# Expert matmuls on column strips while attention runs: one tile shape fewer on TensorE

## The chip, the cores and the metric

The kernel runs on one core of a Trainium2 chip. The metric is the device time of one execution in microseconds (us); three executions of the kernel before took 396.23, 396.54 and 396.64 us, median 396.54. One further execution was taken by the hardware profiler, and all profile lines below are of that one. The engines are named as in the profile: PE is TensorE's matmul, PEld its weight load, DVE is VectorE, ACT is ScalarE, POOL is GpSimd (here it issues the loads), SP is SyncE (here it issues the stores).

## The reference

Eight batches with twelve heads of 448 tokens and 64 dimensions go through attention; the heads are joined to rows of 768, and a feed-forward layer ("expert") with one hidden layer of 2,048 and a SiLU follows.

```python
scores = (1/sqrt(64)) * q @ k.transpose(0, 1, 3, 2)        # [8, 12, 448, 448]
attn = softmax(scores, axis=-1)
x = (attn @ v).transpose(0, 2, 1, 3).reshape(3584, 768)
h = x @ w_in                                                # w_in [768, 2048]
g = h / (1 + exp(-h))
out = g @ w_out                                             # w_out [2048, 768], float32
```

Inputs come and the output goes in float32; the kernel computes in fp16 with sums in float32.

## The kernel before, in words

**Attention.** A unit is one batch and one group of four heads (`HG`); batch 0 is cut in two pieces by query, so there are 27 units of 224 or 448 queries. Keys stand in four chunks of up to 128 (`NCH`). `scores` (line 339) computes keys x queries: each head has 64 dimensions, taken as two times 32 rows, and the four heads of the group use the four row strips of the array, tiles of 32x128. ScalarE takes the exponential from PSUM to an SBUF tile `E` (`expo`, line 359).

448 keys are three chunks of 128 and a rest of 64. From unit 7 on, units are worked in pairs (two groups of heads), and the two rests share one chunk: one group lies `low`, its last 64 keys in rows 0 to 63 of chunk 3, the other `high`, in rows 64 to 127 (`form`, `X_TOK`, lines 186 to 261; `load_v` and `turn_k` place V and K so). Scores of the shared rest use tiles of 32x64 (`scores_rest`).

`attend` (line 414) forms, on tiles of 128x32 with one head on each column strip, first the sums of the exponentials (`part` 0, for pairs in `attend_sums`, line 398, with VectorE's sums `T` of the chunks) and then the values, in two parts of 32 of the 64 dimensions. A part of a pair runs for each of its two groups three chunks x four heads of 128x32, and after both groups the shared rest as eight matmuls of 64x32, one half of the rows for each group. `inverse` and `norm` (lines 438 and 468) then write normalised values to `xT` on VectorE.

**Expert.** `ffn1` (line 484) is 6 matmuls of 128x128 against 448 columns (224 for batch 0) into a PSUM bank `h`; ScalarE takes a tanh and VectorE the gate, into `G` (or `X`). The second layer, `product` (line 675), works on two output tiles of 128 tokens at a time with seven products instead of eight, each 8 matmuls of 128x128 against 384 columns; combinations are formed on VectorE (`combine_g`, `combine_w`). The first four output pieces (two tiles, two halves each) are computed plainly (`plain`, line 695). The last two batches' first layer is done in seven products too (`pair_product`, line 603), with buffers of V and E reused for the combinations (`old_buffer`, line 555).

**Order.** A planner at the end of the kernel (lines 763 to 1500) simulates the engines with costs: each piece of work is an `Op` with a cost and what it depends on, `Order.on_pe` (line 106) adds `SWITCH` (0.094) where the tile mode differs from the one before, and rings stand for buffers (`m_ring` for four PSUM banks, `e_ring` for E, `v_ring` for V). TensorE takes score bursts at a pace of 2.6 us, attention where its data are there, and expert work in between. Emitters are collected with their planned time and called in that order, so the planner's times set the order of every engine's queue, and nothing else. `busy`, `mode` and the lines `mms * mm(nq)` in `run_av` (line 1360) are such costs. POOL's loads have a fixed order, given at lines 801 to 827.

V is a tile from a rotating pool with two buffers (`load_v`, line 264): the first load into a buffer waits until all reads of the batch two before are over.

Of the kernel before, what the change touches and what calls it, by code (L numbers as in the profile page):

```python
# [25 lines left out]
def mm(n):  # L26
    return n / 2400.0 + 0.0026
# [37 lines left out]
class Op:  # L65


    def __init__(self, eng, busy, emit, deps=(), bias=0.0, tail=HOP, then=None):
        self.eng, self.busy, self.emit = eng, busy, emit
        self.deps, self.bias, self.tail, self.then = list(deps), bias, tail, then  # L70
        self.done = None
        self.half = False

    def ready(self):
        return when(self.deps)
# [2 lines left out]
class Order:  # L78


    def __init__(self, shy):
        self.now, self.shy = 0.0, shy
        self.free = {"PE": 1.0, "ACT": 2.1, "DVE": 1.2, "POOL": 1.2}
        self.wait = {"ACT": [], "DVE": []}
        self.pool = []
        self.dma_free = 0.0
        self.out = []
        self.mode = None
        self.busy = {e: 0.0 for e in self.free}

    def add(self, op):
# [4 lines left out]
        self.out.append((self.now, len(self.out), fn))  # L96

    def start(self, op):
        self.emit(op.emit)
        self.free[op.eng] = self.now + op.busy  # L100
        self.busy[op.eng] += op.busy
        op.done = self.now + op.busy + op.tail
        if op.then:
            op.then(op.done)

    def on_pe(self, op, mode):
        gap = SWITCH if mode != self.mode else 0.0
        self.mode = mode
        op.busy += gap
        self.start(op)  # L110
# [55 lines left out]
def kernel(  # L166
# [69 lines left out]

    rawk, rawq, KT, QT, VT, E, T, acc, rdn_t, xT, g_t, ost_t = ({} for _ in range(12))
    sT_t, inv_t = {}, {}  # L240
    pS_t = {}

# [19 lines left out]


    def load_v(b, hg0, hg1, x):
        if b not in VT:
            VT[b] = sb.tile([128, NH, NCH, D], FP16, name=f"V_{b}", tag="V", bufs=2)
        hs = slice(HG * hg0, HG * hg1)
        first, count = X_TOK[form(b, hg0)][x]
        nc.gpsimd.dma_start(  # L269
            out=VT[b][32 * x : 32 * (x + 1), hs, 0:count, :],  # L270
            in_=v[b, hs].rearrange("h (i g) d -> i h g d", g=TPP)[
                :, :, first : first + count, :
            ],
        )
# [37 lines left out]
    def turn_q(n):  # L312
        t = rawq[n][:].bitcast(FP32).rearrange("p (g i) -> p g i", i=32)
        nc.vector.transpose(out=t, in_=t)  # L314
        QT[n] = rawq[n].rearrange("p (q e) -> p e q", e=2)

    def score_banks(n, w, ys):
        for y in ys:
# [63 lines left out]
    def attend_mm(a, n, part, c, h, k0, k1, e, start, stop):  # L382
        b, hg, g0, g1 = units[n]
        nq = 32 * (g1 - g0)
        at = nq * (c % per_burst(n))
        if part == 0:
            w = ones[k0:k1, :]
        else:
            w = VT[b][k0:k1, HG * hg + h, c, part - 1 :: 2]
        nc.tensor.matmul(  # L390
            out=a[32 * h : 32 * (h + 1), 0:nq],
            lhsT=w,
            rhs=e[k0:k1, h, at : at + nq],
            start=start,
            stop=stop,
        )
# [15 lines left out]
                )  # L412

    def attend(ns, part):
        made = []
        lone = len(ns) == 1
        if part == 0 and not lone:
            attend_sums(ns)
            return
        for n in ns:  # L420
            a = ps.tile([128, 512], FP32, name=f"a_{n}_{part}", tag="m", bufs=4)
            made.append(a)
            acc[(n, part)] = a
            for c in range(NCH if lone else NCH - 1):
                for h in range(HG):
                    attend_mm(
                        a, n, part, c, h, 0, rows_of(n, c), E[(n, c // per_burst(n))],
                        c == 0, lone and c == NCH - 1,
                    )
        if not lone:  # L430
            for h in range(HG):
                for i, n in enumerate(ns):
                    attend_mm(
                        made[i], n, part, 3, h, 64 * i, 64 * (i + 1), E[(ns[0], 3)],
                        False, True,
                    )

    def inverse(ns, step, i=0):
# [45 lines left out]
    def ffn1(b, f, t0, t1):  # L484
        h = ps.tile([128, 512], FP32, name=f"h_{b}_{f}_{t0}", tag="m", bufs=4)
        for cc in range(NDC):
            nc.tensor.matmul(  # L487
                out=h[:, 0 : t1 - t0],
                lhsT=w_in_t[:, cc, 128 * f : 128 * (f + 1)],
                rhs=x3(b, cc)[:, cc % 3, t0:t1],  # L490
                start=(cc == 0),
                stop=(cc == NDC - 1),
            )
        h_t[(b, f, t0)] = h
# [108 lines left out]
    def pair_product(f, m):  # L603
        if m in (1, 5):
            pp_t[(f, PBANK[m])] = ps.tile(
                [128, 512], FP32, name=f"f_{f}_{m}", tag="m", bufs=4
            )[:, 0:S]
        elif m == 6:
            two = ps.tile([128, 2, 512], FP32, name=f"f_{f}_{m}", tag="s", bufs=2)
            pp_t[(f, "B")], pp_t[(f, "D")] = two[:, 0, 0:S], two[:, 1, 0:S]  # L610
        x = {(r, i): x3(PB + r, 3 * i) for r in range(2) for i in range(2)}
        lo, at = f // 4 * 4, slice(128 * (f % 4), 128 * (f % 4 + 1))
        a, w = {
            1: (x[0, 0], w_in_part(0, 0, f, f + 1)),
            2: (x[0, 1], w_in_part(1, 0, f, f + 1)),
            3: (sx_t.get(4), w_in_part(1, 1, f, f + 1)),
        }.get(m, (None, None))
        if a is None:
            i = {4: 4, 5: 1, 6: 2, 7: 3}[m]
            a, w = x[1, 1] if m == 4 else sx_t[i], tw_t[(i, lo)][:, :, at]  # L620
        for c in range(3):
            nc.tensor.matmul(  # L622
                out=pp_t[(f, PBANK[m])],
                lhsT=w[:, c, :],
                rhs=a[:, c, :],
                start=(c == 0 and m in (1, 6, 5)),
                stop=(c == 2),
                skip_group_check=True,
            )
# [45 lines left out]
    def product(qd, m):  # L675
        a, b = 2 * qd, 2 * qd + 1
        if m in (5, 6):
            w = S_t[(qd, m - 4)]
        else:
            t, i = {1: (a, 0), 2: (a, 1), 3: (a, 1), 7: (b, 0), 4: (b, 1)}[m]  # L680
            w = rows(t, i)
        if BANK[m] == m:
            pr_t[(qd, m)] = ps.tile([128, 512], FP32, name=f"p_{qd}_{m}", tag="m", bufs=4)
        for f in range(HF):
            nc.tensor.matmul(  # L685
                out=pr_t[(qd, BANK[m])][:, 0:OH],
                lhsT=w[:, f, :],
                rhs=W_[m][:, f, :],
                start=(f == 0 and BANK[m] == m),
                stop=(f == HF - 1),  # L690
                skip_group_check=True,
            )


    def plain(t, j, f0, f1):
        if f0 == 0:
            pr_t[("o", t, j)] = ps.tile([128, 512], FP32, name=f"o_{t}_{j}", tag="m", bufs=4)
        for f in range(f0, f1):
            nc.tensor.matmul(  # L699
                out=pr_t[("o", t, j)][:, 0:OH],  # L700
                lhsT=rows(t, f // HF)[:, f % HF, :],
                rhs=B_[f // HF, j][:, f % HF, :],
# [624 lines left out]
    def av_at():  # L1327
# [12 lines left out]
        for n in ns:  # L1340
            if len(exp_op.get(n, ())) < 2 * NCH // per_burst(n):
                return None
            first = 0.0 if n == ns[0] else (NCH - 1) * mm(S)
            for i, x in enumerate(exp_op[n]):
                c = i // 2 * per_burst(n)
                if len(ns) == 2 and c == NCH - 1:
                    c = 2 * (NCH - 1) - (n != ns[0]) * (NCH - 1)
# [12 lines left out]
    def run_av():  # L1360
# [30 lines left out]
        if part == 0:  # L1391
            after_sums(ns, op, nq)
        else:
# [137 lines left out]
```

## Time and profile before

| what | value |
|---|---|
| median of three executions | 396.54 us |
| profiled execution | 396.11 us |
| its span, first to last instruction | 394.3 us |
| TensorE busy | 387.6 us (98%), 3,679 matmuls |
| VectorE / ScalarE busy | 272.7 us (69%) / 253.6 us (64%) |
| granted TensorE clock | 1.000 |
| first layer `h`, 448 columns (line 487) | 480 matmuls, 353 ns mean |
| second layer products (line 685) | 728 matmuls, 326 to 327 ns mean |
| values, 128x32 at 448 columns (line 390) | 496 matmuls, 354 ns mean |
| values, rest, 64x32 (line 390) | 160 matmuls, 360 ns mean |

Matmuls are pipelined: the mean of one is longer than the time from its start to the next one's start, and a busy PE need not be at its peak. So the prediction goes by starts. An entry such as `128*32 128x448` names the tile (rows x columns of the array) and the moving operand (partitions x columns).

The order in time, as the timeline shows it: batch 0's attention alone, on small pieces, up to 30 us; then first-layer work and scores mixed; the last plain output matmul starts at 75.5 us; the last score matmul at 294.9, the last attention matmul at 305.1; after that TensorE has only expert work, up to the end.

### The profile page before, as it was taken

The page shows a single profiled execution, that of the slowest core. Times are in us where ns is not written, and L with a number is a line of the kernel's source. Part 1 is how long each engine was busy: PE and PEld are TensorE (multiplying, and loading weights), DVE is VectorE, ACT ScalarE, POOL GpSimd, SP SyncE. Part 2 cuts the span into 40 slices and gives each one's busy share as a digit, 9 for nine tenths or more (in the row PEclk, how much of TensorE's full clock was granted, in tenths as well). Part 3 has the DMA queues.
Part 4 walks back from the last instruction along what each step waited for, and adds up shares of the span by engine and source line. Part 5 has one row for each costly group of instructions (what it writes and reads, how often), then busy time and mean ns, then how long its engine had stood idle before and what let it go on. Part 6 is the DMA issues. An engine that isn't in the chain of part 4 may idle for free.

```text
span 394.3 us, 9242 instructions
## 1 busy us (share of the span) xinstructions
PE 387.6 (98%) x3679; PEld 200.0 (51%) x3679; DVE 272.7 (69%) x570; ACT 253.6 (64%) x404; POOL 83.6 (21%) x153
## 2 busy tenths in 40 slices
PE   8999999999999999999999999999999999999995
PEld 7667764443444444554444444444444555555563
DVE  2466676999967588963698576896879945457332
ACT  4988885696871986753974759867685236763221
POOL 7532547215001532330006131600000000000000
PEclk9999999999999999999999999999999999999999
DMA  7999999919033946292016683711100130001343
GB/s 116 204 210 210 162 179 187 154 35 141 13 65 79 148 56 86 50 193 62 2 23 90 116 162 52 98 24 31 51 2 7 33 99 25 2 1 29 95 110 90
DMA packets 35579, 34.43 MB, mean 87 GB/s; under 512 B 11600, under 2 KB 34000, under 8 KB 35536
## 3 DMA queue, kind: packets, MB, share of 16 engines
q0 software_dynamic: 24784, 22.82, 38.7%
q1 hardware_dynamic: 9984, 10.24, 9.6%
q10 hardware_dynamic: 768, 0.79, 0.8%
q8 instruction: 29, 0.48, 0.5%
q14 instruction: 14, 0.11, 0.1%
HBM read 45.61 MB, written 11.01 MB: 144 GB/s over the span
## 4 chain that ended last, share of the span: by engine, by line
PE 91%; DVE 4%; ACT 1%; DMA 1%; issue 1%; ACTq 0%; POOL 0%; DVEq 0%; POOLq 0%
PE p L685 28%; PE h L487 28%; PE s L327 12%; PE a L390 10%; PE f L622 8%; PE o L699 3%; PE a L406 2%; DMA rq<-in_q_dram 1%; DVE tw L598 1%; ACT E L364 1%; PE z L1438 1%; DVE G L533 1%; ACTq L734 0%; DVE S L671 0%; DVE G L671 0%
## 5 line engine op out<-in xcount | busy, mean ns | idle before, releaser
L364 ACT ACTIVATE E<-s 128x896 f16<-128x896 f32 (+1 forms) x172 | 149.9, 915 | 22.6 <-PE s L327 21.2
L487 PE MATMUL h<-xT,w_in_t 128*128 128x448 f16 (+1 forms) x672 | 118.9, 327 | 0.0
L487 PEld LDWEIGHTS <-w_in_t 128*128 128x128 f16 x672 | 61.1, 98 | 54.4 <-issue 18.8
L498 ACT ACTIVATE th<-h 128x448 f16<-128x448 f32 (+1 forms) x112 | 54.3, 495 | 31.6 <-PE h L487 21.5
L533 DVE SCALAR_TENSOR_TENSOR G<-th,h 128x448 f16<-128x448 f16 (+2 forms) x112 | 55.1, 507 | 16.0 <-ACT th L498 14.0
L685 PE MATMUL p<-w_out_t,G 128*128 128x384 f16 x368 | 65.3, 326 | 0.3 <-DVE xT L473 0.2
L685 PEld LDWEIGHTS <-G 128*128 128x128 f16 x472 | 45.3, 98 | 33.4 <-issue 4.0
L269 POOL DMA_DIRECT2D V<-in_v_dram x88 | 48.6, 570 | 57.1 <-PE a L390 43.6
L327 PE MATMUL s<-rq,KT 32*128 32x448 f16 (+4 forms) x864 | 56.7, 340 | 0.6 <-ACT E L364 0.4
L742 ACT COPY ost<-p 128x384 f32<-128x384 f32 x39 | 18.7, 479 | 48.5 <-PE p L685 33.5
L390 PE MATMUL a<-E,V 128*32 128x448 f16 (+3 forms) x864 | 40.6, 335 | 0.0
L473 DVE SCALAR_TENSOR_TENSOR xT<-a,rdn 128x448 f16<-128x448 f32 (+1 forms) x54 | 28.9, 568 | 12.5 <-PE a L390 11.7
L254 POOL DMA_DIRECT2D rq<-in_q_dram x27 | 15.2, 561 | 105.2 <-PE s L327 85.8
L685 PE MATMUL p<-D,S 128*128 128x384 f16 x208 | 37.4, 327 | 0.0
L327 PEld LDWEIGHTS <-KT 32*128 32x128 f16 (+2 forms) x864 | 17.5, 98 | 28.7 <-issue 25.9
L390 PEld LDWEIGHTS <-V 128*32 128x32 f16 (+2 forms) x864 | 18.2, 95 | 22.6 <-issue 15.3
L375 DVE TENSOR_TENSOR T<-T,E 128x1792 f16<-128x1792 f16 x20 | 21.7, 1086 | 11.4 <-ACT E L364 11.4
L685 PEld LDWEIGHTS <-S 128*128 128x128 f16 x208 | 19.4, 98 | 16.2 <-issue 3.1
L375 DVE TENSOR_TENSOR T<-E,E 128x1792 f16<-128x1792 f16 x20 | 21.7, 1083 | 7.8 <-ACT E L364 7.8
L647 ACT ACTIVATE G<-f 128x448 f16<-128x448 f32 x32 | 16.2, 547 | 8.4 <-PE f L622 8.3
L304 DVE STREAM_TRANSPOSE KT<-rk 128x256 f32<-128x256 f32 (+3 forms) x48 | 16.6, 384 | 5.9 <-DMA rk<-in_k_dram 5.8
L314 DVE STREAM_TRANSPOSE rq<-rq 128x448 f32<-128x448 f32 (+1 forms) x27 | 15.3, 570 | 6.0 <-DMA rq<-in_q_dram 5.9
(124 smaller groups left out, 323.6 us busy)
## 6 DMA issues: line engine op xcount, KB each, us to landing
out_dram<-ost SPq DMA_DIRECT2D x208, 48.0 KB, 1.6
rk<-in_k_dram POOLq DMA_DIRECT2D x24, 224.0 KB, 4.9
rq<-in_q_dram POOLq DMA_DIRECT2D x21, 224.0 KB, 5.2
w_in_t<-in_moe_w_in_dram POOLq DMA_DIRECT2D x6, 512.0 KB, 11.6
w_out_t<-in_moe_w_out_dram POOLq DMA_DIRECT2D x4, 768.0 KB, 12.9
V<-in_v_dram POOLq DMA_DIRECT2D x43, 64.0 KB, 3.8
V<-in_v_dram POOLq DMA_DIRECT2D x40, 48.0 KB, 3.6
out_dram<-ost ACTq DMA_DIRECT2D x16, 48.0 KB, 1.8
```

The costliest lines, as they stand in the source:

```text
L269: nc.gpsimd.dma_start(out=VT[b][32 * x : 32 * (x + 1), hs, 0:count, :], in_=v[b, hs].rearrange("h (i g) d -> i h g d", g=TPP)[:, :, first ...
L327: nc.tensor.matmul(out=pS[p0 : p0 + 32 * (x1 - x0), h % 2, at : at + nq], lhsT=KT[(b, hg)][32 * h : 32 * (h + 1), c, x0:x1, :, e], rhs=QT[ ...
L364: nc.scalar.activation(out=E[(n, w)][0:kr, 2 * y : 2 * y + 2, 0:nk], in_=pS_t[(n, w, y)][0:kr, :, 0:nk], func=AF.Exp, scale=attn_scale,)
L375: nc.vector.tensor_tensor(out=T[n], in0=T[n] if step else E[(n, 0)], in1=E[(n, step + 1)], op=ALU.add,)
L390: nc.tensor.matmul(out=a[32 * h : 32 * (h + 1), 0:nq], lhsT=w, rhs=e[k0:k1, h, at : at + nq], start=start, stop=stop,)
L473: nc.vector.scalar_tensor_tensor(out=x3(b, cc)[:, cc % 3, 32 * g0 : 32 * g1], in0=acc[(n, part)][:, 0:nq], scalar=0.5, in1=rdn_t[n].rearra ...
L487: nc.tensor.matmul(out=h[:, 0 : t1 - t0], lhsT=w_in_t[:, cc, 128 * f : 128 * (f + 1)], rhs=x3(b, cc)[:, cc % 3, t0:t1], start=(cc == 0), s ...
L498: nc.scalar.activation(out=th, in_=h_t[(b, f, t0)][:, 0 : t1 - t0], func=AF.Tanh)
L533: nc.vector.scalar_tensor_tensor(out=dst[:, f, at + lo : at + hi], in0=th_t[(b, f, t0)][:, lo - t0 : hi - t0], scalar=1.0, in1=h_t[(b, f, ...
L622: nc.tensor.matmul(out=pp_t[(f, PBANK[m])], lhsT=w[:, c, :], rhs=a[:, c, :], start=(c == 0 and m in (1, 6, 5)), stop=(c == 2), skip_group_ ...
L685: nc.tensor.matmul(out=pr_t[(qd, BANK[m])][:, 0:OH], lhsT=w[:, f, :], rhs=W_[m][:, f, :], start=(f == 0 and BANK[m] == m), stop=(f == HF - 1),
L742: nc.scalar.copy(out=ost(qd, i, j), in_=bank(qd, m))
```

## The change

Three things belong together.

1. While attention lasts and the four plain pieces are done (`od.attention`), `on_pe` gives every operation of mode `full` the mode `cols` and marks it `strips`. The new `wide` then issues each of its 128x128 matmuls as four of 128x32, one on each column strip, with the same moving rows. Before and after that, full matmuls stay.
2. The values of a pair no longer take the rest on 64x32 tiles. Chunk 3 is run as any other, 128 rows deep, for both groups, against the shared `E`; the rows that belong to the other group meet zeros in V. A part of a pair has 32 matmuls as before, but eight steps of four where there were six of four and one of eight.
3. V lies in two fixed buffers. `clear_v` puts the zeros in once, by memsets on VectorE: two at the start, three behind batch 0's values and one behind the first pair's. The loads never write these places again, since a head group of a buffer keeps its form from batch to batch.

The planner's costs follow: 8 instead of 7 matmul times for a part of a pair, no mode `rest cols`, other due times for the exponentials of the rest.

```diff
     def start(self, op):
-        self.emit(op.emit)
+        self.emit(lambda: self.run(op))
...
+    def run(self, op):
+        self.strips = op.strips
+        op.emit()
+
     def on_pe(self, op, mode):
+        if mode == "full" and self.attention:
+            mode, op.strips = "cols", True
         gap = SWITCH if mode != self.mode else 0.0
...
+    VT = [const.tile([128, NH, NCH, D], FP16, name=f"V{i}") for i in range(2)]
+
+    def clear_v(i, hg, low):
+        rows = slice(64, 128) if low else slice(0, 64)
+        nc.vector.memset(VT[i][rows, HG * hg : HG * (hg + 1), NCH - 1], 0.0)
+
+    for hg in (1, 2):
+        clear_v(1, hg, hg == 1)
...
     def load_v(b, hg0, hg1, x):
-        if b not in VT:
-            VT[b] = sb.tile([128, NH, NCH, D], FP16, name=f"V_{b}", tag="V", bufs=2)
...
+    def wide(out, lhsT, rhs, **flags):
+        n = 4 if od.strips else 1
+        for j in range(n):
+            at = slice(128 // n * j, 128 // n * (j + 1))
+            nc.tensor.matmul(out=out[at], lhsT=lhsT[:, at], rhs=rhs, **flags)
...
         for n in ns:
             a = ps.tile([128, 512], FP32, name=f"a_{n}_{part}", tag="m", bufs=4)
-            made.append(a)
             acc[(n, part)] = a
-            for c in range(NCH if lone else NCH - 1):
+            for c in range(NCH):
+                e = E[(ns[0] if c == NCH - 1 else n, c // per_burst(n))]
                 for h in range(HG):
                     attend_mm(
-                        a, n, part, c, h, 0, rows_of(n, c), E[(n, c // per_burst(n))],
-                        c == 0, lone and c == NCH - 1,
-                    )
-        if not lone:
-            for h in range(HG):
-                for i, n in enumerate(ns):
-                    attend_mm(
-                        made[i], n, part, 3, h, 64 * i, 64 * (i + 1), E[(ns[0], 3)],
-                        False, True,
+                        a, n, part, c, h, 0, rows_of(n, c), e, c == 0, c == NCH - 1
                     )
...
     def ffn1(b, f, t0, t1):
...
-            nc.tensor.matmul(
+            wide(
...
-            t = sb.tile([128, NH, NCH, D], FP16, name=name, tag="V", bufs=2)
-            t = t.rearrange("p h c d -> p (h c d)")
+            t = VT[name[:2] == "sx"].rearrange("p h c d -> p (h c d)")
...
-            mms = 7 if two else 4
+            mms = 8 if two else 4
...
-            mms * mm(nq) + 0.013 + (0.03 + SWITCH if two and part else 0.0),
+            mms * mm(nq) + 0.013,
...
                     v_ring.give(at)
+                    i = units[ns[-1]][0]
+                    for hg in range(NG if i == 0 else 1 if i == 1 else 0):
+                        low = i == 0 and hg != 1
+                        od.add(
+                            Op("DVE", 0.2, lambda hg=hg, low=low: clear_v(i, hg, low), [op], 5)
+                        )
...
         od.on_pe(op, "cols")
-        if two and part:
-            od.mode = "rest cols"
...
+        od.attention = bool(qk_seq or av_seq) and len(plain_op) == 4
         soon = od.step()
```

The matmul calls in `pair_product`, `product` and `plain` become `wide` as that in `ffn1` does.

More of the change, by code (lines that the diff above doesn't have):

```diff
@@ L72, in __init__ @@
         self.half = False
+        self.strips = False
     def ready(self):
@@ L88, in __init__ @@
         self.mode = None
+        self.strips = False
+        self.attention = True
         self.busy = {e: 0.0 for e in self.free}
@@ L233 @@
     w_out_t = const.tile([128, NFF, DM], FP16, name="w_out_t")
-    rawk, rawq, KT, QT, VT, E, T, acc, rdn_t, xT, g_t, ost_t = ({} for _ in range(12))
+    VT = [const.tile([128, NH, NCH, D], FP16, name=f"V{i}") for i in range(2)]
[4 more added lines that the diff above has]
+        clear_v(1, hg, hg == 1)
+    rawk, rawq, KT, QT, E, T, acc, rdn_t, xT, g_t, ost_t = ({} for _ in range(11))
     sT_t, inv_t = {}, {}
@@ L269, in load_v @@
         nc.gpsimd.dma_start(
-            out=VT[b][32 * x : 32 * (x + 1), hs, 0:count, :],
+            out=VT[b % 2][32 * x : 32 * (x + 1), hs, 0:count, :],
             in_=v[b, hs].rearrange("h (i g) d -> i h g d", g=TPP)[
@@ L388, in attend_mm @@
         else:
-            w = VT[b][k0:k1, HG * hg + h, c, part - 1 :: 2]
+            w = VT[b % 2][k0:k1, HG * hg + h, c, part - 1 :: 2]
         nc.tensor.matmul(
@@ L414, in attend @@
     def attend(ns, part):
-        made = []
         lone = len(ns) == 1
@@ L621, in pair_product @@
         for c in range(3):
-            nc.tensor.matmul(
+            wide(
                 out=pp_t[(f, PBANK[m])],
@@ L684, in product @@
         for f in range(HF):
-            nc.tensor.matmul(
+            wide(
                 out=pr_t[(qd, BANK[m])][:, 0:OH],
@@ L698, in plain @@
         for f in range(f0, f1):
-            nc.tensor.matmul(
+            wide(
                 out=pr_t[("o", t, j)][:, 0:OH],
@@ L1342, in av_at @@
                 return None
-            first = 0.0 if n == ns[0] else (NCH - 1) * mm(S)
+            first = 0.0 if n == ns[0] else NCH * mm(S)
             for i, x in enumerate(exp_op[n]):
                 c = i // 2 * per_burst(n)
-                if len(ns) == 2 and c == NCH - 1:
-                    c = 2 * (NCH - 1) - (n != ns[0]) * (NCH - 1)
                 deps.append((x, first + c * mm(32 * (units[n][3] - units[n][2]))))
```

## The prediction

> **What bounds the kernel now.** I read the page's first part and its chain first, then TensorE's timeline, then the chain of single stretches.
>
> ```profile
> PE 387.6 (98%) x3679; PEld 200.0 (51%) x3679; DVE 272.7 (69%) x570; ACT 253.6 (64%) x404; POOL 83.6 (21%) x153
> ...
> PE 91%; DVE 4%; ACT 1%; DMA 1%; issue 1%; ACTq 0%; POOL 0%; DVEq 0%; POOLq 0%
> ```
>
> TensorE is on the chain for 91% of the span: whatever shortens its own queue shortens the kernel, unless somebody else becomes late. From the whole chain, the two longest pieces of unbroken full-array work give the price of one matmul:
>
> ```profile
> 323.38 28.37 PE f L622 x150
> 356.06 28.61 PE p L685 x176
> ```
>
> 28.37/150 = 0.1891 us for 448 columns, 28.61/176 = 0.1626 us for 384. Next, TensorE's timeline (start, duration, line, tile shape, count); a duration reaches past the next start, so I go from start to start:
>
> ```profile
> 250.64 0.57 PE L327 MATMUL s<-rq,KT 32*128 32x448 f16 x8
> 251.15 0.56 PE L406 MATMUL a<-T,half 128*32 128x448 f16 x8
> 251.54 0.36 PE L406 MATMUL a<-E,both 128*32 128x448 f16 x4
> 251.83 2.44 PE L487 MATMUL h<-xT,w_in_t 128*128 128x448 f16 x12
> 254.21 0.57 PE L327 MATMUL s<-rq,KT 32*128 32x448 f16 x8
> 254.72 3.19 PE L390 MATMUL a<-E,V 128*32 128x448 f16 x64
> ...
> 299.44 1.46 PE L685 MATMUL p<-w_out_t,G 128*128 128x384 f16 x8
> 300.84 1.63 PE L390 MATMUL a<-E,V 128*32 128x448 f16 x32
> 302.40 1.47 PE L685 MATMUL p<-w_out_t,G 128*128 128x384 f16 x8
> ```
>
> Four 128x32 matmuls on the four column strips run beside each other: I call four of them a step, and a step takes as long as one full matmul. Twelve sum matmuls are 3 steps, 0.567 us, but take 251.83 - 251.15 = 0.68. The 0.113 left over is paid because the tile shape changes. It is paid at every change of shape: 12 h matmuls are 2.269 and take 2.38 (0.111 into the score matmuls); 8 p matmuls are 1.301 and take 1.40 (0.099 into 128x32). One part of a group pair's values (300.84 to 302.40) is 7 steps, 1.324, and takes 1.56: 0.236 for two changes, into the 64x32 tiles of the last keys and out again.
>
> **The change, part by part.** I counted shape changes in TensorE's timeline from the last plain output matmul (75.6) to the last attention matmul (305.4).
>
> A. Sums followed by an expert matmul: 9 times, each saves 0.113: 1.02 us.
> B. Expert matmul followed by sums or values: 9 times 0.099: 0.89.
> C. Values: each of 20 parts (10 pairs) gets one step more (0.189, the zeros in V). In 17 parts both changes go: 0.236 - 0.189 = 0.047 each, 0.80 in all. In three, one change stays (the first pair comes before the new mode, with scores behind its first part and full matmuls behind its second; full matmuls follow the very last part too): 0.118 - 0.189, so -0.21 together.
> D. At the start a plain output matmul is now followed by strips, a new change: -0.10.
> E. Some 60 score bursts keep both their changes. From strips the way out may cost a little more: batch 0's values (0.50 for 4 steps of 0.0959) leave 0.117 against 0.111 from full: 60 x 0.006 = -0.36. Bounds: 0 and, by the way out of the 64x32 tiles (one step of 0.189 that lasts 0.316 start to start, 0.127 over), -1.0.
>
> Together 1.02 + 0.89 + 0.80 - 0.21 - 0.10 - 0.36 = 2.04 us.
>
> F. The strips themselves. In that window stand 480 matmuls of line 487 and 408 of line 685; each becomes four, with four weight loads: 5,328 more instructions. At 448 columns the nearest row is values, 0.189 a step, equal to full. At 384 there is no row. Lower bound 0.1626 (as many columns to stream, so no gain); upper bound the 0.189 of the 448 step. I take 0.1626, for two rows at 224 columns and below: 48 value matmuls in batch 0 take 1.27 for 12 steps, less 0.11 for the change 0.097 a step, against 0.096 full, so a shorter step than ours is still met. In issue a 384 step asks 8 instructions in 163 ns, 20.4 ns each; a group of two products and one score burst (144 instructions in 3.22 us) 22.4. The busy view of batch 0's dense stretch:
>
> ```profile
> 16.00:24.24 8.24, 8.24 (x200) 5.25 (x200) 4.84 (x15) 7.48 (x9) 3.58 (x6) 1.00 1.13 209
> ```
>
> 400 instructions in 8.24 us, 20.6 ns each, with the DMA engines full. What no row shows is four strips reading the same moving rows (attention's four read different heads); I cost that at nothing too, and it belongs to the first rival.
>
> A rule against the change: the Trainium skill's TensorEngine Tiling (Array Packing), Restrictions, says that column tiling switches fast weight loading off; its page TensorE: Matmul & The Clock Gate, LDWEIGHTS, gives columns/1.2 ns, so an estimate of 107 ns for four strips. Beside a 163 ns step that hides; exposed it would be 888 x 0.107 = 95 us. Values, with new weights in every step, show 0.189 a step at 448, so the trace bears out the hidden case there.
>
> G. Clears: two memsets at the start and four in the run. A 128x64 uint32 memset takes 0.11 us, so about 0.15 each. The first two lie in VectorE's 3.17 us idle wait for the first keys. Three follow batch 0's last values (32 us; VectorE is busy 46.6 of the first 75 us), one the first pair (73 us). They wait for the value matmuls; behind them in VectorE's queue stand gates and normalisations, and batch 2's V loads on POOL wait for them. Uncovered they would be 0.6 us. Cost taken: 0.
> H. V in two fixed buffers: POOL waits 43.6 us in 5 waits for value matmuls before a V load, with K and Q loads queued behind. A wait per head group can only end earlier, and TensorE's weight loads name V's transfer as what they waited for in 1.5 us in all. Gain 0. More instruction loads (341 KB in 230 us, one 16 KB block per 5.6 us) ride beside: such blocks are already met every 6 to 7 us between 20 and 38 us.
> I. The planner costs fewer changes and will set some work differently. TensorE's stalls from such order are 0.23 us each now (104.5, 157.6, waiting for ScalarE's copy of a product); I allow three of them, 0.7, either way.
>
> J. What is late next. The chain around the end of attention:
>
> ```profile
> 293.62 0.49 ACT E L364
> 294.13 1.09 DVE T L375
> ...
> 307.38 0.34 DVE S L671
> 307.72 0.55 DVE xT L473
> 308.26 0.04 issue
> 308.31 9.26 PE p L685 x56
> ```
>
> For 14 us VectorE works without a break and TensorE then waits 0.16 us for it. What is saved before 293.6 brings the exponentials and so VectorE's run forward too; what is saved behind it only lengthens the wait. Behind it lie three of B (0.30), one of A (0.11), one part of C (0.05) and the last part (-0.07): 0.39 lost.
>
> Net 2.04 - 0.39 = 1.65 us. The profiled execution took 396.11 (span 394.3), so 394.46; the median shown, 396.54, lies 0.43 above it, and against that the forecast is **394.9**.
>
> **The rivals.**
> First, slower: strips at 384 columns cannot run at 163 ns, by issue or by four readers of the same rows. If 8 instructions take what they take at 448 (23.6 ns each, 189 a step), 408 x 0.0265 = 10.8 us, so 396.54 - 1.65 + 10.8 = 405.7. It decides from 1.65/408 = 4 ns a step, that is above 20.8 ns an instruction. For it: no row at 384, and no long unbroken run of strips. Against: the 20.6 ns above, and 13 ns over the 96 instructions of batch 0's 1.27 us. Chance 0.14, the exposed weight loads included.
> Second, no change: attention's end is set by VectorE and ScalarE, not by TensorE, so the wait at 308 grows by all that was saved: 396.5. For it: VectorE 4.40 and ScalarE 4.74 busy of 5 us at 292 to 297. Against: between 262 and 294 VectorE idles for ScalarE and TensorE nine times, up to 1.55 us. Chance 0.17.
> Third, slower: the sequencer's lead. Matched with the program order, the wait instructions ahead of values (51 ns each, two of them 110 ns apart) are recorded with some 16 matmuls still to start, 3 us of full matmuls but 4 steps, 0.7 us, of strips. An operation released late then needs 6 more instructions issued, 6 x 20.6 = 0.124 us. For one in four of the 131 expert operations (80 of line 487, 51 of 685) that is 4.1 us: 399.0; it decides from 13 operations on. Against: in this window TensorE waits beyond shape changes only three times. Chance 0.09.
> The forecast keeps 0.60.
>
> **How the numbers follow.** The likeliest case's own range: low 394.9 less J (0.39), E (0.36) and 0.7 of order, 393.4; high with E at its -1.0 (0.64 more) and 0.7 of order, 396.2. The range reaches over the second rival to the third's 399.0 and leaves out the first (0.14) and some 0.06 of tails: 393.4 to 399.0. About 0.2% (0.8 us) is what a measurement here can tell from none, so the forecast's upper end counts as no change, with 0.02 of its 0.60: faster 0.58, same 0.19, slower 0.23.
>
> **What would show it.** In the profile after: no 64x32 matmuls; in the window only score bursts change the shape; 128x32 steps of h at 0.189 and of p at 0.163, start to start; sums to expert without the 0.11; the wait at about 306 for the last xT near 0.5 us. A p step of 0.17 or more, or gaps ahead of the first strip of an operation, makes the forecast wrong; so does a wait at 306 of 2 us.

## The result, and the profile after

The changed kernel takes 394.73 us (median of 5 executions, 394.58 to 394.84); the kernel before, on the same chip, 396.23 (395.79 to 396.64). The ratio is 0.9967, with a 95% interval of 0.9955 to 0.9978: 1.5 us, or 0.33%, faster. In the groups of runs below five executions of the kernel before came out at 410 to 412 us, at a granted clock of 0.95 to 0.96, and its medians and the ratios leave them out. The profiled execution took 394.84 us, span 392.9; that of before 396.11, span 394.3.

From the page of the changed kernel, TensorE's busy time and number of matmuls, the queue that loads instructions (packets, MB, share), and the chain by engine:

```profile
PE 386.2 (98%) x6343; PEld 213.1 (54%) x6343; DVE 274.1 (70%) x576; ACT 253.1 (64%) x404; POOL 83.6 (21%) x153
...
q8 instruction: 49, 0.80, 0.9%
...
PE 95%; DVE 2%; ACT 1%; ACTq 0%; issue 0%; DVEq 0%
```

There are 2,664 more matmuls, and TensorE is busy for 1.4 us less. So four 128x32 matmuls cost no more than the full one that they replace, and the bound is where it was: on TensorE, now for 95% of the span. Another price stands in the second line: 49 blocks of instructions of 16 KB where there were 29.

TensorE's timeline of the changed kernel, around the same sums and near the end of attention (start, duration, line, tile, moving operand, count):

```profile
249.56 0.57 PE L349 MATMUL s<-rq,KT 32*128 32x448 f16 x8
250.06 0.56 PE L428 MATMUL a<-T,half 128*32 128x448 f16 x8
250.45 0.36 PE L428 MATMUL a<-E,both 128*32 128x448 f16 x4
250.64 2.44 PE L337 MATMUL h<-xT,w_in_t 128*32 128x448 f16 x48
253.02 0.57 PE L349 MATMUL s<-rq,KT 32*128 32x448 f16 x8
253.52 3.21 PE L412 MATMUL a<-E,V 128*32 128x448 f16 x64
256.56 0.74 PE L337 MATMUL h<-xT,w_in_t 128*32 128x448 f16 x12
...
299.23 1.69 PE L412 MATMUL a<-E,V 128*32 128x448 f16 x32
300.75 1.47 PE L337 MATMUL p<-w_out_t,G 128*32 128x384 f16 x32
302.05 1.69 PE L412 MATMUL a<-E,V 128*32 128x448 f16 x32
303.67 2.77 PE L337 MATMUL p<-D,S 128*128 128x384 f16 x16
306.88 0.32 PE L337 MATMUL p<-w_out_t,G 128*128 128x384 f16 x1 [0.45 <-DVE xT L486]
```

The sums now run from 250.06 to 250.64: 0.58 us for 3 steps, where it was 0.68. One part of a pair's values, 299.23 to 300.75, is 1.52 for 8 steps, where it was 1.56 for 7. The product behind it, 300.75 to 302.05, is 1.30 for 8 steps, where it was 1.40. No 64x32 tile is left. The last line is the bill: TensorE now idles 0.45 us for the last `xT`, where it idled 0.16, as the timeline of the kernel before shows:

```profile
308.31 1.46 PE L685 MATMUL p<-w_out_t,G 128*128 128x384 f16 x8 [0.16 <-DVE xT L473]
```

The chain of the changed kernel around that wait (start, duration, engine, tile, line):

```profile
302.22 1.54 PE a L412 x32
303.76 0.04 issue
303.80 0.42 DVE G L683
304.23 1.74 DVE tw L610 x2
305.96 0.34 DVE S L683
306.30 0.55 DVE xT L486
306.84 0.04 issue
306.88 3.25 PE p L337 x19
```

In these 3.04 us, 303.80 to 306.84, VectorE alone sets the pace: gates, two combinations of weights `tw` and a sum stand ahead of the last `xT` in its queue. In the chain of before VectorE's run stretched over some 14 us; now only its last three microseconds are on it.

**Where the time came from.** TensorE's operations stand in the same order in both programs, so the lead of the changed kernel can be followed operation by operation, as the difference of two starts. At 68 us, ahead of the first pair's values, it is 0.03 us. The first pair's two parts already have the extra step, among expert matmuls that are still full, and take it to -0.10 at 75 us; the first change of shape takes it to -0.19. It is 1.76 at 302, 1.71 when the last part of values is over, and 1.42 behind the wait for `xT`. From there to the end it moves by 0.02 at most; the spans differ by 1.4. So 1.68 us were gained between 68 us and the end of values, and 0.29 of them were lost in the wait, which leaves 1.39. A second run of the changed kernel (below) gives 1.69 and 0.28 in the same places.

### The profile page after: what moved, and what is told of

Same layout as the page of the kernel before. It is cut to its first block, busy times and chain, and to the rows that moved or that the text cites. A ratio compares the mean times of both kernels' runs of the same rounds, so it can differ in the third digit from the quotient of the medians.

```text
span 392.9 us, 14583 instructions
## 1 busy us (share of the span) xinstructions
PE 386.2 (98%) x6343; PEld 213.1 (54%) x6343; DVE 274.1 (70%) x576; ACT 253.1 (64%) x404; POOL 83.6 (21%) x153
## 4 chain that ended last, share of the span: by engine, by line
PE 95%; DVE 2%; ACT 1%; ACTq 0%; issue 0%; DVEq 0%
PE h L337 29%; PE p L337 28%; PE s L349 13%; PE a L412 10%; PE f L337 8%; PE o L337 3%; PE z L1452 2%; PE a L428 2%; ACT E L386 1%; DVE p L758 1%; DVE tw L610 0%; ACTq L746 0%; DVE T L397 0%; ACT ost L754 0%; DVE rdn L470 0%
## 5 line engine op out<-in xcount | busy, mean ns | idle before, releaser
L337 PE MATMUL h<-xT,w_in_t 128*32 128x448 f16 (+1 forms) x2112 | 119.3, 345 | 0.0
L337 PEld LDWEIGHTS <-w_in_t 128*32 128x32 f16 (+1 forms) x2184 | 72.8, 97 | 56.7 <-issue 16.4
L337 PEld LDWEIGHTS <-G 128*32 128x32 f16 (+1 forms) x1352 | 54.5, 97 | 36.3 <-issue 5.2
L337 PE MATMUL p<-w_out_t,G 128*32 128x384 f16 (+1 forms) x1016 | 65.5, 326 | 0.7 <-DVE xT L486 0.4
L412 PE MATMUL a<-E,V 128*32 128x448 f16 (+2 forms) x864 | 41.2, 333 | 0.0
L337 PE MATMUL p<-D,S 128*32 128x384 f16 (+1 forms) x544 | 37.5, 327 | 0.0
L412 PEld LDWEIGHTS <-V 128*32 128x32 f16 (+1 forms) x864 | 21.5, 97 | 16.5 <-issue 4.1
L337 PEld LDWEIGHTS <-S 128*32 128x32 f16 (+1 forms) x544 | 20.7, 97 | 14.9 <-issue 2.3
L337 PE MATMUL p<-D,G 128*32 128x384 f16 (+1 forms) x272 | 19.1, 326 | 0.0
```

Source lines behind the costliest of these rows:

```text
L337: nc.tensor.matmul(out=out[at], lhsT=lhsT[:, at], rhs=rhs, **flags)
L412: nc.tensor.matmul(out=a[32 * h : 32 * (h + 1), 0:nq], lhsT=w, rhs=e[k0:k1, h, at : at + nq], start=start, stop=stop,)
```

## The experiments

All ratios are to the kernel before on the same chip, whose medians were 395.95, 395.94 and 395.95 us in the three groups of runs.

### One half at a time

The strips without the zeros in V: everything of the change except that V's rest keeps its 64x32 tiles and V its rotating buffers.

```diff
-                    a, n, part, c, h, 0, rows_of(n, c), e, c == 0, c == NCH - 1
+                    a, n, part, c, h, 0, rows_of(n, c), E[(n, c // per_burst(n))],
...
+        if not lone:
+            for h in range(HG):
+                for i, n in enumerate(ns):
+                    attend_mm(
+                        made[i], n, part, 3, h, 64 * i, 64 * (i + 1), E[(ns[0], 3)],
```

> The strips without the zeros: the shared rest keeps its 64x32 tiles and V its rotating pool. Theory (time is steps plus about 0.1 us for every change of tile shape): 9 changes sums to expert (0.106 each in the changed kernel's trace) and 9 expert to attention (0.104) go, one at the start is added (0.09), 57 exits into scores cost 0.010 more each: 0.95 + 0.94 - 0.09 - 0.57 = 1.2 us, of which about 0.4 falls behind VectorE's last run and is lost in the wait: 0.8 to 1.2 us below the kernel before. Rival (the gain comes from the values on whole 128-row tiles, the strips are only neutral): no difference from the kernel before.

Measured: 395.0 us (394.54 to 395.14), ratio 0.9971 (0.9961 to 0.9982): by the ratio 1.15 us below before, within what was expected.

The zeros in V without the strips: all expert matmuls stay full.

```diff
-        od.attention = bool(qk_seq or av_seq) and len(plain_op) == 4
+        od.attention = False
```

> The zeros in V and the fixed buffers alone; expert matmuls stay 128x128. Theory: 5 parts of values that are followed by more values save two changes and add a step (0.047 each), 15 parts save only one change (0.118 - 0.189 = -0.071): 0.24 - 1.07 = 0.8 us slower than the kernel before, a little less where the wait at the end shrinks. Rival (this part carries the gain): 1 to 1.5 us faster than before.

Measured: 396.67 us (396.35 to 397.27), ratio 1.0016 (1.0007 to 1.0025): this half alone is slower, by 0.6 us. TensorE's timeline of this kernel shows both prices still being paid:

```profile
251.79 0.36 PE L428 MATMUL a<-E,both 128*32 128x448 f16 x4
252.08 2.44 PE L337 MATMUL h<-xT,w_in_t 128*128 128x448 f16 x12
254.46 0.57 PE L349 MATMUL s<-rq,KT 32*128 32x448 f16 x8
```

From the last sums to the full matmul it takes 0.29 (252.08 - 251.79) where strips follow after 0.19 (250.64 - 250.45). A part followed by a full matmul lost 0.065 us against before, one followed by another part or other work on column strips gained 0.05. By the ratios, the two halves alone come to -1.15 + 0.63 = -0.5 us; the whole change gives -1.3 (0.0033 x 396), and -1.1 in a second run of it below. So the strips alone bring most of it. The zeros cost 0.6 us without them; what they bring with them is more than these times can tell. The traces tell a little more: followed as above, from 68 us to behind the wait for the last `xT`, the strips alone gain 0.97 us and the whole change 1.39 and 1.40 in its two runs. The extra step pays only where both changes of shape around it go, and they go only if the expert work has the same shape.

### Is it the shape, or the smaller pieces?

Strips of 128x64, two for each matmul: the same order of work, but the shape differs from attention's again.

```diff
     def wide(out, lhsT, rhs, **flags):
-        n = 4 if od.strips else 1
+        n = 2 if od.strips else 1
```

> As the changed kernel, with the same order on every engine, but the marked expert matmuls come as two of 128x64 instead of four of 128x32. Theory: what counts is that the shape stays the same as attention's; with 128x64 the changes are back, A, B and all but five of C are lost, so as the zeros alone: about 0.8 us slower than the kernel before, 2.3 us slower than the changed one. Rival (column tiling of any width lets matmuls follow attention's without a drain): as the changed kernel, 1.5 us faster than before.

Measured: 397.76 us (397.55 to 398.29), ratio 1.0045 (1.0033 to 1.0058): 1.8 us slower than before, a microsecond more than expected. TensorE's timeline of this kernel, at the same sums:

```profile
252.48 0.56 PE L428 MATMUL a<-T,half 128*32 128x448 f16 x8
252.87 0.36 PE L428 MATMUL a<-E,both 128*32 128x448 f16 x4
253.16 2.46 PE L337 MATMUL h<-xT,w_in_t 128*64 128x448 f16 x24
```

The sums take 253.16 - 252.48 = 0.68 us again, as before the change. So what the change saves is the price of a change of tile shape, about 0.1 us each (0.10 to 0.12 here), and cutting a matmul into pieces is no gain by itself. The microsecond not expected is this shape's own. The first step of two 128x64 after a change takes 213 ns to the next start where a full matmul takes 200 (187 and 173 at 384 columns), and the way out into scores 288 where it takes 285. With 69 such entries and 60 ways into scores that is 0.9 + 0.2 = 1.1 us.

### Strips further out: to the end

If strips cost nothing, they should cost nothing behind attention either.

```diff
-        od.attention = bool(qk_seq or av_seq) and len(plain_op) == 4
+        od.attention = len(plain_op) == 4
```

> As the changed kernel, but strips go on to the end of the program: 320 more matmuls at 384 columns and 168 at 448 become four each, in unbroken runs of over a hundred steps. Theory (a step of four strips costs what a full matmul costs): within 0.3 us of the changed kernel; one change of shape less, but it lies ahead of the wait for VectorE. Rival (issue of 8 instructions in 163 ns cannot be held over long runs): with 21 ns an instruction 168 ns a step, 320 x 5 ns = 1.6 us slower than the changed kernel, and more at a slower issue.

Measured: 395.67 us (395.05 to 397.75), ratio 0.9995 (0.9984 to 1.0007): all the gain but 0.2 to 0.3 us is gone. That is about a microsecond above the changed kernel, where 0.3 at most was expected. The profiled execution happened to be the fastest of them all, 395.05, and its trace shows little; so the same kernel was run again, beside the changed kernel.

> The changed kernel itself, beside the others of this set on the same chip: 1.3 to 1.7 us faster than the kernel before, as in its first measurement (ratio 0.9967).

> Strips up to the end of the program once more. In its first measurement it stood at 0.9995 of the kernel before, with equal steps in its trace (0.189 and 0.162 to 0.163) but longer waits at hand-overs to the other engines. Theory (strips cost nothing by themselves): 0.3 us or less above the changed kernel beside it. Rival (where no attention is left, strips have no change of shape to save and each hand-over costs them something, in issue or in results that come later): again 0.7 to 1.2 us above the changed kernel.

Measured: the changed kernel 394.82 us (394.45 to 395.58), ratio 0.9973 (0.9964 to 0.9982); strips to the end 395.84 (395.45 to 396.59), 0.9998 (0.9989 to 1.0007). The loss is real. It isn't in the steps, as the chain of strips to the end shows in its longest unbroken stretch:

```profile
321.98 28.51 PE f L337 x600
...
386.92 1.27 ACTq L746
```

600 strips are 150 steps in 28.51 us, where 150 full matmuls took 28.38; a step takes 0.189 here too, but for six that take 0.215. The second line is a store issued by ScalarE's queue: 1.27 us. In the chain of the changed kernel run beside it the same store is 0.37. Of the 1.16 us lost behind 303 us, 0.22 are lost by the start of TensorE's last step, and 0.93 behind it, with the last stores. ScalarE's timeline of strips to the end, near its end (copies out of PSUM, then issues of stores):

```profile
384.74 0.48 ACT L754 COPY ost<-p 128x384 f32<-128x384 f32 x1 [0.59 <-PE p L337]
385.25 3.43 ACTq L746 DMA_DIRECT2D out_dram<-ost  x4
388.80 0.48 ACT L754 COPY ost<-p 128x384 f32<-128x384 f32 x1 [3.58 <-issue]
```

Four issues take 3.43 us, and the copy behind them waits for the issuing alone. One issue takes 0.31 to 0.44 us in an undisturbed stretch. The long ones stand beside a packet that brings a block of instructions: in this run packets begin 13.29 and 7.76 us before the end, and the issues at 13.3 and 7.1 before the end take 1.5 and 1.3 us on both issuing engines. Other runs agree: before has a block at 10.86 us from its end and two issues of 1.22 and 1.29 there; the zeros without strips at 10.88, with 1.41 and 1.47; strips of 128x64 at 7.76, with 1.60 and 1.66. The changed kernel has no block there, and all its issues take 0.31 to 0.44. In the fast execution of the first run the last two blocks, 12.84 and 6.76 us before the end, met one long issue, of 1.17 on SyncE and none on ScalarE. Over all thirteen traces 155 of 2,912 store issues take more than 1 us, up to 2.5, and 154 of them overlap a packet of a block; but 194 others overlap one and stay under 1 us. Nor does each long one cost time: those of the kernel before did not move the lead.

That gave a forecast that can fail: strips behind attention, but full matmuls for the last 112 products, so that the end of the program needs no block, should give the changed kernel's time.

```diff
-        od.attention = bool(qk_seq or av_seq) and len(plain_op) == 4
+        od.attention = len(plain_op) == 4 and (bool(qk_seq or av_seq) or len(moe) > 14)
```

> Strips after attention too, but not for the last two pairs of output tiles (the last 112 products, some 18 us). Theory (strips to the end were 1 us slower because more instruction blocks are loaded during the last stores, and a store's issue that meets such a load takes 1.2 to 1.6 us instead of 0.43): back to within 0.4 us of the changed kernel, 1.0 to 1.6 us faster than before. Rival (hand-overs from strips to the other engines are dearer all along the tail): most of the loss stays, 0.2 to 0.7 us faster than before.

Measured: 394.95 us (394.71 to 395.4), ratio 0.9973 (0.9962 to 0.9984): the changed kernel's time. ScalarE's timeline at the same place:

```profile
385.04 0.48 ACT L754 COPY ost<-p 128x384 f32<-128x384 f32 x1 [1.58 <-PE p L337]
385.55 2.49 ACTq L746 DMA_DIRECT2D out_dram<-ost  x4
388.16 0.48 ACT L754 COPY ost<-p 128x384 f32<-128x384 f32 x1 [2.63 <-PE p L337]
```

The four issues fit into 2.49 us, none takes more than 0.44, and the copy waits for TensorE. That a late instruction block and a slow store issue go together is shown in these runs. Why they do, whether the issue waits for the block's packet or for a memory path that both use, isn't.

### Strips further out: from the start

Strips from the first expert matmul on, so in batch 0 too, where a matmul has 224 columns. The planner's order is left as it was.

```diff
+        self.always = True
...
-        if mode == "full" and self.attention:
-            mode, op.strips = "cols", True
+        if mode == "full":
+            op.strips = self.always or self.attention
+            mode = "cols" if self.attention else mode
...
+        od.always = bool(qk_seq or av_seq)
```

> As the changed kernel and in its order, but strips from the first expert matmul on: 192 matmuls at 224 columns and the 64 plain ones at 384 become four each too. Theory A (weight loads stay hidden at 224 columns, a step is 96 ns as batch 0's values show behind their first step): seven changes more go and the added one at the start too, 8 x 0.105 = 0.8 us, less 14 exits at 0.01: 0.7 us faster than the changed kernel. Theory B (at 224 columns four weight loads of 26.7 ns each, an estimate by the Trainium skill's TensorE: Matmul & The Clock Gate, LDWEIGHTS, do not fit under 96 ns; a step is 107 ns): 192 x 11 ns = 2.1 us lost, so 1.4 us slower than the changed kernel.

Measured: 406.73 us (405.46 to 407.17), ratio 1.0265 (1.0249 to 1.0281). Neither theory was near: this is 12 us above the changed kernel. TensorE's timeline of this kernel:

```profile
32.04 0.27 PE L339 MATMUL h<-xT,w_in_t 128*32 128x224 f16 x4
34.05 1.24 PE L339 MATMUL h<-xT,w_in_t 128*32 128x224 f16 x44 [1.74 <-issue]
35.22 0.57 PE L351 MATMUL s<-rq,KT 32*128 32x448 f16 x8
35.73 2.00 PE L339 MATMUL h<-xT,w_in_t 128*32 128x224 f16 x76
39.97 1.24 PE L339 MATMUL h<-xT,w_in_t 128*32 128x224 f16 x44 [2.24 <-issue]
```

Where it runs, a step of 224 columns takes 96 ns, as a full matmul of that size does. But five times TensorE stands still, waiting for nothing that the profile shows: 12.3 us in all by the view of waits, as much as the whole loss. Counted in order through TensorE's own program, weight loads and matmuls alike, the five places are instructions 1218, 1474, 1730, 2242 and 2498, each 194 above a multiple of 256, and 256 instructions are one block of 16 KB. Block packets start at 31.81, 37.75, 43.67, 47.21, 54.29 and 60.90 us, 3.5 to 7.1 us apart, and TensorE goes on some 2.2 to 2.5 us after one starts. So it is out of instructions. A step of 96 ns takes eight of them, 12 ns each, so a block is used up in 3 us. The DMA engines are full meanwhile, their share 1.12 in 28 to 65 us.

If that is right, the strips have nothing to do with it. Full matmuls, cut by columns into pieces of 56, need instructions as fast. Here batch 0's 192 first-layer matmuls are cut so; four accumulations then share one bank, so that batch 0's hidden values aren't kept whole, and what is computed from them is another result.

```diff
+            if b == 0:
+                for c0 in range(0, t1 - t0, 56):
+                    nc.tensor.matmul(
+                        out=h[:, c0 : c0 + 56],
+                        lhsT=w_in_t[:, cc, 128 * f : 128 * (f + 1)],
+                        rhs=x3(b, cc)[:, cc % 3, t0 + c0 : t0 + c0 + 56],
```

> The changed kernel, but each of batch 0's 192 full first-layer matmuls (128x128 against 224 columns) comes as four full matmuls against 56 columns each, with no column strips: as many TensorE instructions there as strips from the first expert matmul on had, on the old tile shape. Theory (instruction loading: with the DMA engines full a block of 256 instructions arrives about every 6 us, and 12 ns an instruction uses it up in 3): five waits of 2 to 3.3 us, each 194 places behind a multiple of 256 in TensorE's program, 12 to 15 us slower than the changed kernel. Rival (strips at 224 columns are slow in themselves): at most 2 us slower, by 192 x 4 x 2.5 ns of fixed time.

Measured: 408.95 us (406.97 to 409.21), ratio 1.0318 (1.0297 to 1.0339), 14.1 us above the changed kernel's 394.82: within what was expected of instruction loading. TensorE's timeline of the kernel with pieces of 56 columns:

```profile
34.16 1.30 PE L502 MATMUL h<-xT,w_in_t 128*128 128x56 f16 x44 [1.45 <-issue]
35.39 0.57 PE L349 MATMUL s<-rq,KT 32*128 32x448 f16 x8
35.89 2.14 PE L502 MATMUL h<-xT,w_in_t 128*128 128x56 f16 x76
40.08 1.30 PE L502 MATMUL h<-xT,w_in_t 128*128 128x56 f16 x44 [2.05 <-issue]
```

The waits stand at the same five places, each 194 above a multiple of 256: 9.9 us in five by the view of waits. They are shorter than expected, 1.45 to 2.6 us where 2 to 3.3 were, so the sum is met in part by luck: of the rest, some 2.6 us are the granted clock, 0.93 in 28 to 65 us (an estimate, 0.07 x 37). So the wait belongs to the number of instructions, not to the tile shape. The Trainium skill's Runtime: NRT & Kernel Launch, section "Instruction fetch mechanics", says that blocks of 256 instructions are fetched ahead and that crossing a block's border is mostly hidden; at 20 to 24 ns an instruction these traces agree. At 12 ns beside full DMA engines they don't. One more such place shows in all thirteen kernels, before included: at 28 us, at place 961, 193 above such a multiple, among batch 0's sums, whose steps of 96 ns ask for 12 ns an instruction too, 0.06 to 0.65 us are lost. Whether 12 ns would do with idle DMA engines wasn't tried.

A middle way follows from this: strips from the end of batch 0's first layer on, at 58 us, so that the plain pieces (384 columns) are strips as well.

```diff
-        od.attention = bool(qk_seq or av_seq) and len(plain_op) == 4
+        od.attention = bool(qk_seq or av_seq) and all(len(g_op.get((0, f), ())) == 2 for f in range(NFF))
```

> Strips from the end of batch 0's first layer on, that is for the four plain output pieces too, with the planner told so. Theory (a change of shape costs about 0.105 us wherever it stands): three from plain output to attention, one back and the added one at the start go, 5 x 0.105 = 0.5 us, less some exits: 0.4 us faster than the changed kernel. Rival (at this point the other engines set the pace, VectorE is busy 4.0 to 5.0 of 5 us from 64 to 109 us, and the gain is waited away): no difference from the changed kernel.

Measured: 394.33 us (394.08 to 394.6), ratio 0.9961 (0.9948 to 0.9973): 1.6 us below before and 0.5 below the changed kernel beside it, as expected in size, though the two intervals overlap. The view of stretches (length, then busy time and count of PE, PEld, DVE, ACT and POOL, granted clock, DMA share, GB/s):

```profile
58.00:75.10 17.10, 17.10 (x382) 9.02 (x384) 13.21 (x23) 10.05 (x15) 9.85 (x18) 1.00 1.21 199
```

766 instructions in 17.1 us are 22 ns each, with the DMA engines fuller than ever, and TensorE doesn't idle at all. This is the best version found.

### The wait for the last xT

Could the wait at 306 be taken away? On top of the last version, the two combinations of weights ahead of the last `xT` on VectorE are held back until it is done.

```diff
+            if f0 == 4 and (PB + 1, NDC - 1, 0) not in x_op:
+                return
+            last = [x_op[(PB + 1, c, 0)] for c in (3, 5)] if f0 == 4 else []
...
-                    [pair_w[(k, f0)] for k in {2: (1,), 4: (2,)}.get(m, ())],
+                    [pair_w[(k, f0)] for k in {2: (1,), 4: (2,)}.get(m, ())] + last,
```

> Strips from the end of batch 0's first layer on (as in the run with the early start), and in addition the combinations of w_in for the second half of the pair products wait for the last xT, so that VectorE normalises first and the PSUM banks come free. Theory (the wait of 0.45 us at 306 is for VectorE's two combinations of 0.87 us ahead of the last xT): 0.3 to 0.5 us faster than with the early start alone, so 2.0 to 2.3 us faster than before. Rival (VectorE has no break until 316, what is put off comes due there): no difference from the early start, 1.5 to 1.8 us faster than before.

Measured: 394.86 us (394.37 to 394.94), ratio 0.9969 (0.9956 to 0.9981): nothing gained. TensorE's timeline of this kernel:

```profile
305.79 1.46 PE L337 MATMUL p<-w_out_t,G 128*128 128x384 f16 x8
...
317.60 0.73 PE L337 MATMUL f<-xT,w_in_t 128*128 128x448 f16 x3 [0.63 <-ACT G L659]
```

There is no wait at 306 any more, and one of 0.63 us at 317.6, for ScalarE. The planner also sets another piece of first-layer work there (`f<-xT,w_in_t`), which stood further back without this edit. So what was saved at 306 was lost again eleven microseconds later. Whether that lies in VectorE's combinations, which now come later, or in this other order isn't shown.

## Why the prediction was right

It said 394.9; it is 394.73. The mechanism held, and most terms were met, but that the numbers agree this closely is partly luck. The forecast stands on a median of 396.54 before, which came out as 396.23 over five executions; the gain was forecast as 1.65 and is 1.50 by the medians, 1.3 by the ratio (1.1 in the second run) and 1.39 in the trace. A little less gain and a little faster start cancel.

- **A, B and D.** Taken 0.113, 0.099 and 0.10 each. By the lead, eight of the nine changes of A gave 0.106 and one 0.088, 0.94 in all. Eight of B gave 0.093 to 0.108, and the ninth, ahead of the last sums at 297.6, gave 0.005: TensorE waits for VectorE there in both kernels, 0.34 us from the last h matmul to the first sum, which the prediction had counted as a change of shape like the others. So B is 0.80 where 0.89 was taken. D cost 0.094. Shown by strips of 128x64 too, which put the prices back.
- **C.** Taken 0.047 a part; measured 0.044 to 0.054 by the lead. The first pair's parts lost 0.065 each and the last 0.051, together 0.18 where 0.21 was taken. As a difference of whole times, the 0.6 us of this term isn't shown: the strips without the zeros came within 0.2 us of the whole change.
- **E was mis-sized.** Taken at 0.006 a burst, 0.36 in all. From strips into scores it takes 295 ns where it took 285 from full matmuls (at 384 columns 268 and 259), so 0.010 at each of 60 bursts, 0.60. The row chosen for it, batch 0's values at 224 columns, was the wrong neighbour. The way in is 0.003 shorter at 47 of them, which gives 0.14 back; by the lead the term is some 0.45.
- **F.** Strips take 0.189 at 448 columns and 0.163 at 384, the full matmul's price. The first rival, 10.8 us for slower strips, is out, and with it the exposed weight loads that it included. The Trainium skill's TensorEngine Tiling (Array Packing), Restrictions, says that column tiling disables fast weight load. The 128x32 strips lose nothing by it: even at 224 columns, in the strips from the start, a step takes 96 ns, as a full matmul of that size does, and less than the 107 that the prediction estimated for four weight loads one after the other. Why they fit isn't shown.
- **G and H.** The clears hide, as taken. GpSimd's waits for value matmuls before V's loads, 43.6 us before, are gone and gained nothing, as taken. That more instruction blocks ride beside the work held in this kernel, with 49 of them. The prediction's "one 16 KB block per 5.6 us" is not the added 341 KB, which make one per 11 us, but near the rate of all blocks there, one per 6 us (38 from 75.5 to 305.5 us). It was a narrower margin than the prediction knew: strips from the start and strips to the end both broke it.
- **I.** No order changed on TensorE up to the end of attention. Of the 0.7 us allowed for stalls from timing, one came: a product at 122.5 us starts when an addition on VectorE is over, 452 ns from the step before to its start. The lead falls by 0.136 there, where this part of C would have raised it by 0.05: 0.19 lost.
- **J.** 0.39 us was to be lost in the wait for the last `xT`; 0.29 were (0.45 of idle time against 0.16), since the change of B at 297.6, one of those counted for it, had gained nothing. The second rival, that all would be waited away there, is out: the wait took a sixth of the lead. Holding back what stands ahead of that `xT` brought nothing, since another wait followed eleven microseconds further on; how much VectorE has to spare behind attention isn't shown by that.

The sum. Taken: 2.04 up to the end of values, less 0.39, so 1.65. By the lead: from 0.03 to 1.71, so 1.68, less 0.29, so 1.39. The 0.36 missing up to the end of values are A (0.08), B (0.09), E (0.09) and the stall at 122.5 (0.19), with small gains of some 0.09 against them; J gave 0.10 back. The third rival, 4.1 us from operations that find TensorE's sequencer late, didn't come. Two expert operations are released late by ScalarE in both kernels, at 104.6 and 157.6 us, and start 0.015 later behind the change, not 0.124. What a reader behind the strips does lose is small: from the start of the last matmul of an operation to the reader's start it takes 403 to 406 ns, where it took 389 behind full ones.

## What to carry to other kernels

Where pieces of work on different tile shapes alternate on TensorE, count the changes of shape: each costs about a tenth of a microsecond, and giving the larger work the shape of the smaller one saves it, as long as four strips together still take no longer than one full matmul. The price is four times the instructions; work out nanoseconds per instruction, stretch by stretch, and keep such cutting out of stretches where a step is short and the DMA engines are full, and out of the end of the program, where the last stores are issued.

## What was not expected of the hardware

- **TensorE can run out of instructions.** At 12 ns an instruction, with a DMA share of 1.12, it stood still for 1.4 to 3.1 us at single places 256 instructions apart, 10 to 12 us in all, whatever the tile shape; at 20 to 24 ns, with a share of up to 1.21, it didn't.
- **A store's issue can triple.** On ScalarE's and SyncE's queues it mostly takes 0.31 to 0.44 us, and, in 154 cases over all traces, 1.0 to 2.5 us where a packet with a block of instructions goes by. In the strips to the end some 0.9 us of that was on the path.
- **Two strips aren't half of four.** At 448 columns the first step after a change of shape takes 213 ns on 128x64 tiles, and 200 on full ones and on 128x32.
